# Another split of the pairs that take three cycles: ten, two and five, seven products

## The chip, the core and the metric

The kernel runs on one NeuronCore of a Trainium2 chip. Its engines run side by side and wait for each other through semaphores: PE (matmul, with its weight loads listed apart as PEld), DVE (vector), ACT (scalar), POOL (general purpose) and SP, whose queue issues the DMAs. The metric is the time of one execution on the device in microseconds, lower is better. Three runs of the kernel before took 1713.72, 1713.96 and 1714.29 us; the median is 1713.96 us.

## What is computed

The input is one sequence of 2048 tokens with 512 features, all in f32. The reference, cut to what matters:

```python
xn = _layernorm(x)
qkv = (xn @ wqkv) -> q, k, v of 32 heads, 16 wide each
scores = einsum("bhqd,bhkd->bhqk", q, k) * 16 ** -0.5
s = (softmax(scores) @ v, heads side by side) @ wo            # attention over all 2048 keys
h = (xn @ w_gate) * (xn @ w_up)                               # 1792 wide
g = silu(h @ w_down)
out = x + s * g
```

## The kernel before

**Two streams of work on PE.** The attention is cut into 32 units (8 groups of four heads by 4 chunks of 512 queries), each with 16 tiles of 128 keys. One *position* is one head of one key tile of one unit: there are 2048. A position (`position`, `expo`, `score`) issues two matmuls: `t`, the scores that are exponentiated on ACT into a tile `e`, and `s`, the scores of the position 86 later, turned the other way round, of which DVE takes the row maxima with one `tensor_reduce` (`mx`). The two use 64 rows of PE's array each, one the lower and one the upper half, and run side by side.

The second stream is everything else that PE must do once the first unit runs: projections of q and k, the gated layer and its down projection. These come as *pairs* (`pair`): two sums of products, each accumulated in a PSUM bank of its own (`misc`, two banks). A matrix product in split precision is a list of terms; 12 terms for one result at a contraction of 512, 15 for a down projection over five blocks of 128 features. The contraction of each term is cut in two halves of 64 rows: the lower half for one result runs beside the upper half for the other. One such step of two matmuls is called a *product* here (one `yield 1`). A pair has two halves of 12 or 15 products. In the first, the lower rows go to result 0 and the upper rows to result 1; in the second it is the other way round. So that the two halves of the array do not write the same bank at once, a one-element ACT copy (`look`, L294) reads result 1 between the two halves: the first product of the second half waits for it.

**Cycles.** The program is laid out by a planner in the Python code, and the order on every engine is the order of the program. A *cycle* takes two key tiles of a unit through: some positions, products between them, and then a *block* (`block`, L645), the matmuls `pv` that multiply the exponentials of eight positions with V; they use 128 rows and 32 columns each. ACT copies the block's result out (`part` at L656, `acc` at L651 for the first block of a unit). There are 256 cycles; 240 of them carry pairs.

**Banks.** PSUM has eight: three for `s`, three for `t` and the block's result together (tag `st`), two for `misc`. They are given out in turn. A position's `s` therefore needs the reduce of the position three before to be done. Behind a block the order of tag `st` is block, t of place 0, t of place 1, t of place 2, t of place 3: the t of place 2 needs the block's result copied out, and the t of place 3 needs the exponential of place 0 done. Place 0 is the first position of a cycle.

**The planner** is the class `Filler`. `fetch` runs when a half of a pair begins; for the first half it asks how many cycles the pair gets (`spread(n)`, 2 to 4, by the share of all products) and fills `queue` with the number of products of each cycle. With three cycles the middle one holds the end of the first half and the start of the second, as a tuple (`split`, `more`). `begin` takes the next entry; the main loop then chooses the number of positions:

```python
fits = min(9, max(7, int(2.6 + 0.62 * work))) if q + LEAD < TOTAL and work else 8
need = 8 * (b + 1)
last = min(max(q + fits, need + AHEAD[0]), need + AHEAD[-1], TOTAL - 4)
```

so that positions run one to four ahead of what the block needs. `Filler.spread` makes `plan`, the number of products behind each position of the cycle; `part` issues them. `share(n, gaps)` spreads n evenly, larger shares first. Between cycles `values` issues what reads the finished pair out of its banks (`before_values`: one DVE multiply for the gated layer at L357; two DVE additions, L428, for the down projection of the second and third group of blocks, one copy for the first), then the block, then what POOL has to split.

`soon`, `step` and `later` delay loads, splits and the silu by a count of positions, not of products.

Of the kernel before, what the change touches and what calls it, by code (L numbers as in the profile page):

```python
# [48 lines left out]
def body(ctx, tc, x, wqkv, wo, wg, wu, wd, out):  # L49
# [62 lines left out]
    def banks_of(bufs):  # L112
        stack = ExitStack()
        fst["ps"] = stack.enter_context(tc.tile_pool(name="ps" + "".join(bufs), bufs=1, space=PSUM, reuse_waits="tile")), bufs
        return stack
# [15 lines left out]
    def flush():  # L131
        while waiting:
            waiting.pop(0)[1]()
# [8 lines left out]
    def run_all(queue):  # L142
        while queue:
            queue.pop(0)()
# [309 lines left out]
    def prepare():  # L454

        done = [(NG - 1) * NC + c in finished for c in range(NC)]
        if 0 not in ops:
            if done[0] and fst.get("wo") == ND - 1:
                o_split(0, small_tiles())
        for c in (1, 2):  # L460
            if c not in ops and done[c] and ("big", c) in fst:
                h, l = fst["big", c]
                o_split(c, [(h[:, d], l[:, d]) for d in range(ND)])
        if 3 not in ops and "first" in fst:
            o_split(3, small_tiles())
# [171 lines left out]
    def block(todo):  # L637

        i = todo[0][0]
        g = i // NC  # L640
        o = psum("st", f"pv{i}")
        for n, (_, kt, es) in enumerate(todo):
            for j in range(4):
                h0 = (4 * g + j) * VW
                nc.tensor.matmul(o[32 * j:32 * j + 32], V[:, kt, h0:h0 + 32], es[j],  # L645
                                 start=n == 0, stop=n == len(todo) - 1)
        if todo[-1][1] == NT - 1 and i == NU - 1:
            last_heads(o)
        elif todo[0][1] == 0:
            sums[i] = keep.tile([P, 512], F32, name="acc", bufs=2)  # L650
            nc.scalar.activation(sums[i], o, AF.Copy)  # L651
        elif now[0] > NU * NT - LEAD // 4:
            nc.vector.tensor_tensor(sums[i], o, sums[i], op=OP.add)
        else:
            part = part_tile()
            nc.scalar.activation(part, o, AF.Copy)  # L656
            pool.tensor_tensor(sums[i], sums[i], part, op=OP.add)
# [43 lines left out]
    def run(gen):  # L701
        for _ in gen:
            pass
# [105 lines left out]
    def filler(wq0):  # L809
        yield from proj_pair(0, [(wq0, 0, 2), (wq0, 0, 3)])  # L810
        for m in range(1, NG // 2):
            wk, wq = fst["qk", m]
            for c in range(NC):
                if c == 2 and m + 1 < NG // 2:
                    fst["qk", m + 1] = qk_weights(m + 1, 1), qk_weights(m + 1, 0)
                yield from proj_pair(m, [(wk, 1, c), (wq, 0, c)])
                if m == 1 and c:
                    after = fst["high"].ins.name
                    for n, src in enumerate((xh, xl)):
                        put = sync.dma_start(XD[c][n].bitcast(F32), src[c].bitcast(F32))  # L820
                        tc.add_manual_dep(put.ins, after, BEHIND, reason="not before the first exponentials")
                if m == NG // 2 - 1 and c == NC - 2:
                    nxt = gu_weights(0)
        run_all(before_values)
        run_all(behind_values)
        flush()
        qkv.close()
        fst["fp"] = ffp.enter_context(tc.tile_pool(name="ffn", bufs=1, reuse_waits="tile"))
        yield from ffn(nxt)
# [5 lines left out]
    def step_small(q):  # L835
        if q and next(q[0], 1):
            q.pop(0)

    class Filler:
# [11 lines left out]
        def fetch(self):  # L851
            v = next(self.gen, self)
            if v is self:
                self.done = True
            elif v:
                k, n = v
                self.left = n
                if k == 0:
                    self.whole, odd = divmod(self.cycles(2 * n), 2)
                    self.split = max(2, round(n / (2 * self.whole + 1))) if odd else 0  # L860
                    self.more = max(2, self.split - 1) if odd and self.whole else n if odd else 0
                    self.queue = self.share(n - self.split, self.whole) if self.whole else []
                    if odd:
                        self.queue.append((self.split, self.more))
                    if self.whole:
                        self.queue += self.share(n - self.more, self.whole)
# [7 lines left out]
            return sum(both)  # L874

        def spread(self, gaps):
            if isinstance(self.now, tuple):
                a, b = self.now
                self.plan = self.share(a, 2) + [0] + self.share(b, gaps - 3)
            else:  # L880
                self.plan = self.share(self.now, gaps)

        def part(self):
            n = self.plan.pop(0) if self.plan else 0
# [14 lines left out]
    def values(rounds):  # L899
        if before_values:  # L900
            run_all(before_values)
        else:
            step_small(heads)
        run_all(reduced)
        block(rounds)
        run_all(behind_values)
        if rounds[-1][1] == NT - 1:
            heads.append(finish(rounds[0][0]))
            step_small(heads)
# [3 lines left out]
    def position(q):  # L913

        n, j = divmod(q, 4)
        i, kt = divmod(n, NT)
        g, c = divmod(i, NC)
        now[0] = n
        Tied.on = n < 18
        if j == 0:  # L920
            if kt == 8 and i + 2 < NU:
                load_q(i + 2)
            if kt == 0 and g + 1 < NG and c == 1:
                load_k(g + 1)
            ready[n] = i, kt, []
        if j == 3 and kt % 4 == 2:
            gates.append(lambda: step_small(later))
        ready[n][2].append(expo(i, kt, j))
        scored = q + LEAD
        if scored < TOTAL:  # L930
            score(scored, 1)
        step()
        if j == 1:
            prepare()
        if scored < TOTAL and scored % (4 * NT) == 4 * NT - 1:
            reduced.append(lambda: maxima(scored // (4 * NT)))
# [3 lines left out]
    with tc.manual_schedule(engines=ORDERED):  # L940
        with banks_of(EARLY_BUFS):
            fil = Filler(filler(early()), spread)
        ctx.enter_context(banks_of(BUFS))
        run(fst["v"])
        q = 0
        while q < 4:
            position(q)
            q += 1
        for b in range(NU * NT // 2):
            if fil.done:  # L950
                parts = iter([3, 2, 3, 2, 2, 2, 1, 2])
                fil = Filler(ending(), lambda n: next(parts))
            work = fil.begin()
            if b >= NU * NT // 2 - 2:
                last = TOTAL - 4 * (NU * NT // 2 - 1 - b)
            else:
# [3 lines that stand above are left out]
            count = last - q  # L960
            fil.spread(max(2, count - 2))
            for k in range(count):
                if k == count - 1:
                    run_all(gates)
                position(q)
                q += 1
                if 0 < k < count - 1 or count < 3:
                    fil.part()
            if b < NU * NT // 2 - 1:
                values([ready.pop(2 * b), ready.pop(2 * b + 1)])  # L970
        run_all(before_values)
        run_all(gates)
        while heads:
            step_small(heads)
        block([ready.pop(NU * NT - 2), ready.pop(NU * NT - 1)])
        run_all(behind_values)
        flush()
        while fil.left or not fil.done:
            now[0] += 1
            prepare()  # L980
            if not fil.left:
                fil.fetch()
            for _ in range(fil.left):
                next(fil.gen)
            fil.left = 0
            fil.fetch()
            flush()
# [17 lines left out]
```

## Time and profile before

| | |
|---|---|
| median of three runs | 1713.96 us |
| the profiled execution | 1715.28 us |
| its span, first to last instruction | 1713.4 us |
| ACT busy | 1309.0 us, 76% |
| POOL busy | 884.9 us, 52% |
| DMA, mean over the span | 85 GB/s |

The profile shows one execution. In a timeline a row is: start in us, duration in us, engine, source line, operation, output <- input, shapes, count; equal instructions that follow each other are merged into one row with the time from the first start to the last end, or for back-to-back ones their sum. In brackets stands how long the engine sat idle before and what ended it. Matmuls of 512 columns are listed with about 0.39 us each but follow each other on one half of the array every 0.23 us, since they are pipelined; PE's busy share says little for that reason, and the distance between starts says much.

### The profile page before, as it was taken

To read this page: it belongs to the slowest core of one execution; us is meant where nothing else is said; L and a number is where in the kernel's file an instruction comes from. 1 tells how busy PE (TensorE), PEld (TensorE's weight loads), DVE (VectorE), ACT (ScalarE), POOL (GpSimd) and SP (SyncE) were. 2 spreads that over 40 slices of the span, in tenths; PEclk is the share of its full clock that TensorE was granted. 3 is DMA by queue.
4 is the path that set the end of the run, shared out by engine and by line. 5 is a ranking of instruction groups with operands and counts; after the bars stand their busy time and mean duration, and the time that the engine had idled before them with its cause. 6 is when DMAs were issued, how large, how long until landed. Compare 5 with 4: busy or idle time off the path is not lost. (4 is left out here: it accounts for less than half of the span.)

```text
span 1713.4 us, 35012 instructions
## 1 busy us (share of the span) xinstructions
PE 1701.9 (99%) x13574; PEld 1043.7 (61%) x13574; DVE 1430.9 (84%) x2478; ACT 1309.0 (76%) x2568; POOL 884.9 (52%) x890
## 2 busy tenths in 40 slices
PE   8999999999999999999999999999999999999998
PEld 5666656666666666666656665666666566666655
DVE  6788888888888888888888888888888888888933
ACT  6357777777877778788777887877778787777774
POOL 5314444763653647446354572663637546446672
PEclk9999999999999999999999999999999999999999
DMA  6316633620241222412115220330225112011352
GB/s 209 108 40 193 248 126 117 153 72 13 71 91 36 82 72 67 96 41 61 36 49 136 65 72 24 87 76 27 60 84 122 54 36 73 27 54 47 123 178 78
DMA packets 117378, 145.79 MB, mean 85 GB/s; under 512 B 12636, under 2 KB 74332, under 8 KB 114524
## 3 DMA queue, kind: packets, MB, share of 16 engines
q1 hardware_dynamic: 117212, 143.55, 29.0%
q8 instruction: 107, 1.75, 0.4%
q14 instruction: 59, 0.48, 0.1%
HBM read 95.94 MB, written 47.45 MB: 84 GB/s over the span
## 5 line engine op out<-in xcount | busy, mean ns | idle before, releaser
L612 DVE TENSOR_REDUCE mx<-s 128x1 f32<-128x512 f32 x2048 | 1256.1, 683 | 212.4 <-PE s L610 178.1
L634 ACT ACTIVATE e<-t 128x512 f32<-128x512 f32 x2048 | 1101.3, 601 | 97.8 <-PE pv L645 46.6
L632 PE MATMUL t<-qs,ks 50*128 50x512 f32 x2048 | 782.3, 408 | 0.1
L610 PE MATMUL s<-ks,qs 48*128 48x512 f32 x2048 | 768.1, 409 | 0.6 <-DVE mx L612 0.5
L63 POOL TENSOR_TENSOR acc<-acc,part 128x512 f32<-128x512 f32 x214 | 276.1, 1290 | 588.8 <-ACT part L656 588.4
L632 PEld LDWEIGHTS t<-qs,ks 50*128 50x128 f32 x2048 | 359.2, 185 | 270.7 <-issue 110.2
L645 PE MATMUL pv<-e,V 128*32 128x512 f32 x4096 | 492.5, 598 | 0.0
L610 PEld LDWEIGHTS s<-ks,qs 48*128 48x128 f32 x2048 | 350.8, 185 | 28.2 <-issue 5.6
L656 ACT ACTIVATE part<-pv 128x512 f32<-128x512 f32 x214 | 128.1, 599 | 205.1 <-PE pv L645 205.1
L645 PEld LDWEIGHTS pv<-e,V 128*32 128x32 f32 x4096 | 107.0, 109 | 242.3 <-issue 216.9
L290 PE MATMUL g<-fh,w1h 64*128 64x512 f32 x224 | 90.5, 404 | 0.0
L286 PE MATMUL u<-fh,w0h 64*128 64x512 f32 x224 | 90.5, 404 | 0.0
L290 PE MATMUL y<-dh,hh 64*128 64x512 f32 x224 | 89.5, 400 | 0.0
L286 PE MATMUL y<-dh,hh 64*128 64x512 f32 x224 | 88.9, 397 | 0.0
L290 PE MATMUL u<-fh,w0l 64*128 64x512 f32 x224 | 88.2, 394 | 0.0
L290 PE MATMUL g<-fl,w1h 64*128 64x512 f32 x224 | 88.1, 393 | 0.0
L286 PE MATMUL u<-fh,w0l 64*128 64x512 f32 x224 | 88.0, 393 | 0.0
L290 PE MATMUL g<-fh,w1l 64*128 64x512 f32 x224 | 88.0, 393 | 0.0
L286 PE MATMUL g<-fl,w1h 64*128 64x512 f32 x224 | 88.0, 393 | 0.0
L286 PE MATMUL g<-fh,w1h 64*128 64x512 f32 x224 | 87.9, 392 | 0.0
L290 PE MATMUL u<-fl,w0h 64*128 64x512 f32 x224 | 87.8, 392 | 0.0
L286 PE MATMUL g<-fh,w1l 64*128 64x512 f32 x224 | 87.8, 392 | 0.0
(262 smaller groups left out, 2982.7 us busy)
## 6 DMA issues: line engine op xcount, KB each, us to landing
w1r<-in_wg_dram SPq DMA_DIRECT2D x56, 256.0 KB
w0r<-in_wu_dram SPq DMA_DIRECT2D x56, 256.0 KB
wdr<-in_wd_dram SPq DMA_DIRECT2D x56, 256.0 KB
qs<-QD SPq DMA_DIRECT2D x64, 192.0 KB
ks<-KD SPq DMA_DIRECT2D x12, 768.0 KB
KD<-hl SPq DMA_DIRECT2D x16, 512.0 KB
QD<-hl SPq DMA_DIRECT2D x16, 512.0 KB
OD<-acc SPq DMA_DIRECT2D x31, 256.0 KB
```

The lines of the kernel that those rows point to most:

```text
L63: got = getattr(self.engine, name)(*args, **kw)
L286: nc.tensor.matmul(outs[k], l[LOWER], r[LOWER], start=k == 0 and n == 0, stop=(stop or k == 0) and n == len(low) - 1, skip_group_check=k == 1)
L290: nc.tensor.matmul(outs[1 - k], l[UPPER], r[UPPER], start=k == 0 and m == 0, stop=(stop or k == 0) and m == len(high) - 1, skip_group_chec ...
L610: nc.tensor.matmul(o, QS[i][b:b + KB, pr, t * P:(t + 1) * P], k[b:b + KB, pr, kc * 512:(kc + 1) * 512], start=True, stop=True)
L612: nc.vector.tensor_reduce(MX[i][:, j, t, kc:kc + 1], o, axis=AX.X, op=OP.max)
L632: nc.tensor.matmul(o, k[b:b + KR, pr, kt * P:(kt + 1) * P], QS[i][b:b + KR, pr], start=True, stop=True)
L634: nc.scalar.activation(e, o, AF.Exp, scale=DH ** -0.5)
L645: nc.tensor.matmul(o[32 * j:32 * j + 32], V[:, kt, h0:h0 + 32], es[j], start=n == 0, stop=n == len(todo) - 1)
L656: nc.scalar.activation(part, o, AF.Copy)
```

## The change

The numbers of products of the three cycles, and the places of the products in the middle cycle, are changed. For a pair with 12 products a half: before 8, then 4 and 3, then 9; after 10, then 2 and 5, then 7. With 15: before 10, then 5 and 4, then 11; after 12, then 3 and 6, then 9. In the middle cycle the rest of the first half stood behind the second and third position, with one place free before the second half; now it stands whole behind the first position, two places are left free, so that three positions lie between the halves. For that, products may now be issued behind the first position too; plans that do not want it begin with a 0, which gives them the order that they had. Pairs of two and of four cycles keep theirs.

```diff
                 if k == 0:
                     self.whole, odd = divmod(self.cycles(2 * n), 2)
-                    self.split = max(2, round(n / (2 * self.whole + 1))) if odd else 0
-                    self.more = max(2, self.split - 1) if odd and self.whole else n if odd else 0
+                    self.split = 0 if not odd else n if not self.whole else 2 if n < 15 else 3
+                    self.more = 0 if not odd else n if not self.whole else (n - 2) // 2 if n < 15 else n * 2 // 5
                     self.queue = self.share(n - self.split, self.whole) if self.whole else []
...
         def spread(self, gaps):
-            if isinstance(self.now, tuple):
-                a, b = self.now
-                self.plan = self.share(a, 2) + [0] + self.share(b, gaps - 3)
+            if not isinstance(self.now, tuple):
+                self.plan = [0] + self.share(self.now, gaps)
+            elif self.now[0] < 4:
+                self.plan = [self.now[0], 0, 0] + self.share(self.now[1], gaps - 2)
             else:
-                self.plan = self.share(self.now, gaps)
+                self.plan = [0] + self.share(self.now[0], 2) + [0] + self.share(self.now[1], gaps - 3)
...
-                if 0 < k < count - 1 or count < 3:
+                if k < count - 1:
                     fil.part()
```

## The prediction

> **What bounds the kernel now.** I read the page first, then the list of waits, then the timeline of single cycles.
>
> ```profile
> span 1713.4 us, 35012 instructions
> ...
> PE 1701.9 (99%) x13574; PEld 1043.7 (61%) x13574; DVE 1430.9 (84%) x2478; ACT 1309.0 (76%) x2568; POOL 884.9 (52%) x890
> ...
> L612 DVE TENSOR_REDUCE mx<-s 128x1 f32<-128x512 f32 x2048 | 1256.1, 683 | 212.4 <-PE s L610 178.1
> L634 ACT ACTIVATE e<-t 128x512 f32<-128x512 f32 x2048 | 1101.3, 601 | 97.8 <-PE pv L645 46.6
> ```
>
> PE has almost no gap, and DVE's largest idle time is spent waiting for PE. So a cycle lasts as long as PE's steps in it, plus whatever PE waits. The list of waits shows the one that the change moves:
>
> ```profile
> PEld u L286 <- ACT look L294: 5.8, 25, 0.2
> PEld y L286 <- ACT look L294: 3.6, 16, 0.2
> PEld p L286 <- ACT look L294: 1.4, 6, 0.2
> ```
>
> 25 + 16 + 6 = 47 waits; by the planner's arithmetic 48 pairs take three cycles before the ending (35 with 12 products a half, 13 with 15). One such middle cycle, four and three products, in the timeline (`pv` begins a block):
>
> ```profile
> 764.34 1.93 PE L645 MATMUL pv<-e,V 128*32 128x512 f32 x16
> ...
> 766.20 0.50 PE L632 MATMUL t<-qs,ks 50*128 50x512 f32 x1
> ...
> 766.39 0.60 ACT L656 ACTIVATE part<-pv 128x512 f32<-128x512 f32 x1 [1.35 <-PE pv L645]
> 766.54 0.39 PE L632 MATMUL t<-qs,ks 50*128 50x512 f32 x1
> ...
> 766.77 3.68 DVE L612 TENSOR_REDUCE mx<-s 128x1 f32<-128x512 f32 x6 [1.29 <-PE t L632]
> ...
> 766.89 1.57 ACT L634 ACTIVATE e<-t 128x512 f32<-128x512 f32 x3
> ...
> 768.18 0.40 PE L632 MATMUL t<-qs,ks 50*128 50x512 f32 x1
> 768.32 0.14 ACT L294 ACTIVATE look<-u 1x1 f32<-1x1 f32 x1
> ...
> 768.53 0.18 PEld L286 LDWEIGHTS u<-fh,w0h 64*128 64x128 f32 x1 [0.23 <-ACT look L294]
> 768.53 0.49 PE L286 MATMUL u<-fh,w0h 64*128 64x512 f32 x1
> ...
> 768.87 0.39 PE L286 MATMUL u<-fl,w0h 64*128 64x512 f32 x1
> ...
> 769.57 0.39 PE L610 MATMUL s<-ks,qs 48*128 48x512 f32 x1
> 769.89 0.16 PEld L645 LDWEIGHTS pv<-e,V 128*32 128x32 f32 x8 [0.37 <-ACT e L634]
> ```
>
> The look runs behind three exponentials, ends at 768.46, and 0.07 us later the weight load starts. A matmul whose weights load late is listed from the load, but the next one on that half follows after 0.34 us, not 0.23: it counts as started 0.11 later. Without the wait the second product would have stood at 768.18 + 2 x 0.23 = 768.64; it stands at 768.87. **One stall costs 0.23 us.**
>
> Block starts around other kinds of cycle give their lengths:
>
> ```profile
> 708.84 1.92 PE L645 MATMUL pv<-e,V 128*32 128x512 f32 x16
> 714.23 1.93 PE L645 MATMUL pv<-e,V 128*32 128x512 f32 x16
> ...
> 725.77 1.92 PE L645 MATMUL pv<-e,V 128*32 128x512 f32 x16
> 732.04 1.92 PE L645 MATMUL pv<-e,V 128*32 128x512 f32 x16
> 738.11 1.93 PE L645 MATMUL pv<-e,V 128*32 128x512 f32 x16
> 744.84 1.92 PE L645 MATMUL pv<-e,V 128*32 128x512 f32 x16
> 751.81 1.92 PE L645 MATMUL pv<-e,V 128*32 128x512 f32 x16
> 758.78 1.49 PE L645 MATMUL pv<-e,V 128*32 128x512 f32 x12
> ...
> 769.89 1.92 PE L645 MATMUL pv<-e,V 128*32 128x512 f32 x16
> 775.94 1.50 PE L645 MATMUL pv<-e,V 128*32 128x512 f32 x12
> ```
>
> By the plan these are: 7 products with 7 positions, 5.39 (708.84 to 714.23); 10 with 8, 6.27; five and four with 8, 6.07; 11 with 9, 6.73; 12 with 9, 6.97; then 8 with 7, 5.56 (758.78 to 764.34); four and three with 7, 5.55; 9 with 8, 6.05. A step more costs 0.23 (8 with 7 against 12 with 9: six steps, 1.41). So a cycle of n steps takes about 2.08 + 0.233 n: 14 steps want 5.34. The middle cycle of 12 loses 0.21, that of 15 (17 steps, 6.04 wanted) 0.03, the cycle of 7 with 7 loses 0.05. **All that the change can take away is 35 x 0.21 + 13 x 0.03 = 7.7 us, or 0.45%.**
>
> **The change part by part.** The number of positions, products and blocks stays; over three cycles 12-pairs keep 22 positions (8, 7, 7 for 7, 7, 8). No DMA is moved against the positions, since loads and splits are delayed by counts of positions; SP's and POOL's queues keep their order. The plans of all other cycles keep theirs, as the leading 0 issues nothing; these edits cost nothing.
>
> *The look.* It now comes behind the first exponential alone. On ACT it takes 0.05 us of its turn (768.32 to the next exponential, by the spacing of the first three: 1.57 less 0.60, halved, is 0.49); the exponential of place 1 has its scores later than that, which hides it. Counted from the first position (766.20 is 0): exponential 0 runs from 0.69 to 1.29, so the look ends near 1.32, and the second half's first product may load from 1.39. It would stand behind place 3, not before 1.5. So this stall goes.
>
> *What is late next.* With two products behind place 0, PE's steps stand at 0.34 and 0.57 (products), 0.81, 1.04 and 1.27 (places 1, 2, 3). Place 3 needs the reduce and the exponential of place 0. What such a wait costs is seen in a cycle with few products, 7 with 8 positions, that runs into DVE:
>
> ```profile
> 722.21 4.28 DVE L612 TENSOR_REDUCE mx<-s 128x1 f32<-128x512 f32 x7 [0.67 <-PE s L610]
> ...
> 724.15 0.18 PEld L610 LDWEIGHTS s<-ks,qs 48*128 48x128 f32 x1
> 724.15 0.50 PE L610 MATMUL s<-ks,qs 48*128 48x512 f32 x1
> ...
> 724.49 0.39 PE L290 MATMUL y<-dl,hh 64*128 64x512 f32 x1
> ...
> 725.35 0.18 PEld L610 LDWEIGHTS s<-ks,qs 48*128 48x128 f32 x1
> ```
>
> Reduces follow each other every (4.28 - 0.68) / 6 = 0.60. The third ends at 722.21 + 1.20 + 0.68 = 724.09, and place 5's load starts at 724.15; the fifth ends at 725.29, and place 7's starts at 725.35: 0.06 behind the reduce both times, and 0.11 more until the matmul counts. So a place cannot count as started before the end of the reduce (or exponential) three places back plus 0.17.
>
> *Middle cycle of 12.* Reduce 0 runs from 0.57 to 1.25, exponential 0 to 1.29: place 3 counts from 1.46, against 1.27. Loss 0.19. Later places are not held: reduce 1 starts when its scores are there, 0.46 behind place 1 (0.57 less the 0.11 of a late load), at 1.27, ends at 1.95, allows place 4 at 2.12, and that comes at 1.46 + 3 x 0.23 = 2.16; place 6 is allowed at 3.32 and comes at 3.33. Eight steps and 0.32 to the block (769.57 to 769.89): 1.46 + 1.87 + 0.32 = 3.65, with the 1.86 before the first position (764.34 to 766.20) **5.51**, against 5.55. Bounds: 5.34 with no wait; 5.60 if the late restart hits both halves of the array one after the other (another 0.1). I take 5.51, since both releases are rows.
>
> *12-pair.* Before 5.56 + 5.55 + 6.05 = 17.16; after 6.27 + 5.51 + 5.39 = 17.17 by these rows, and 17.14 by the line 2.08 + 0.233 n with the losses 0, 0.17 and 0.05. The first cycle's kind comes as 6.25 to 6.27, so I take -0.02. **35 x -0.02 = -0.7 us** (bounds: 5.34 makes it -6.6, 5.60 makes it +2.5).
>
> *Middle cycle of 15.* Products at 0.34, 0.57, 0.81, places 1 to 3 at 1.04, 1.28, 1.51, two products, place 4 wanted at 2.21, one, place 5 at 2.68, two, place 6 at 3.38, one, place 7 at 3.85, the block at 4.17. DVE has only reduce 0 until place 1's scores come at 1.50; it then runs 1.50, 2.10, 2.70, 3.30. Place 4 counts from 2.18 + 0.17 = 2.35 (+0.14), place 5 from 2.78 + 0.17 = 2.95 (+0.27), place 7 from 3.98 + 0.17 = 4.15 (+0.30). The cycle takes 1.86 + 4.15 + 0.32 = **6.33** against 6.07. Bounds 6.03 and 6.45. With the first and last cycle: before 6.27 + 6.07 + 6.73 = 19.07, after 6.97 + 6.33 + 6.05 = 19.35; by the line, +0.24. I take 0.26: **13 x 0.26 = +3.4 us** (bounds -0.5 and +4.9).
>
> *The end of a pair.* A shorter last cycle leaves DVE less time before the next pair wants the banks. Where two additions must empty them, before:
>
> ```profile
> 613.61 1.92 PE L645 MATMUL pv<-e,V 128*32 128x512 f32 x16
> ...
> 614.78 1.28 DVE L428 TENSOR_TENSOR y<-y,y 128x512 f32<-128x512 f32 x2
> ...
> 620.74 1.49 PE L645 MATMUL pv<-e,V 128*32 128x512 f32 x12
> ```
>
> That pair ended with 9 products and 8 positions, and the cycle behind it took 7.13, not 6.97: 0.16 lost. After the change the eight 15-pairs of the second group end in just that cycle; before, they ended in 11 products, 0.47 later, and lost little. The four 12-pairs of the third group end with 7 and 7, 0.06 worse. **8 x 0.15 + 4 x 0.06 = +1.4 us** (bounds 0 and 2.0). The pairs of the gated layer have one multiply and stay covered.
>
> **The sum:** -0.7 + 3.4 + 1.4 = **+4.1 us**: 1719.4 for the profiled execution of 1715.28, which lies 1.3 above the median; on the median 1718.1, I say **1718**.
>
> *A rule against the change.* The granted clock stays whole over cycles with such short waits:
>
> ```profile
> 700.00:780.00 80.00, 80.00 (x660) 48.55 (x658) 69.16 (x118) 63.42 (x127) 32.83 (x33) 1.00 0.29 61
> ```
>
> Behind the five engines stands the clock, 1.00. The Trainium skill, "TensorE: Matmul & The Clock Gate", section "A second HAM failure mode: psum-queue depth-cycling", tells of a kernel with 512 columns whose short waits on PSUM banks made the clock swing between half and full. By that rule the new waits at place 3 would bring half clock; by the row they do not, and the sum stands.
>
> **The rivals.**
> 1. *The banks are free in time* (faster). If place 3 finds reduce 0 and exponential 0 done, the look's stall goes and nothing takes its place: -6.6 - 0.5 + 1.4 = -5.7, 1708. For it: the wait at the look is a real one. Against it: reduce 0 would have to end 0.15 earlier and exponential 0 0.19 earlier than in the rows. It decides as soon as place 3 comes at 1.46 or later.
> 2. *Waits add up on both halves* (slower by more): 2.5 + 4.9 + 2.0 = +9.4, 1723. For it: the 15-pairs' middle cycle has three waits; against it: in the rows above the other half ran on.
> 3. *A draw*: the 15-pairs' middle cycle, whose pattern no row shows, waits only once, 6.17 in place of 6.33; +4.1 - 2.1 = +2.0, 1716. For it: DVE idles up to 1.50 and has room.
> 4. *Half clock* during the middle cycles: 14 x 0.233 = 3.3 us more in each of 48, +157 us, 1871. The row's 1.00 speaks against it.
>
> That the change does nothing is excluded by the plan: other numbers are issued.
>
> **How the numbers follow.** My forecast 0.53, rival 1 0.12, rival 2 0.16, rival 3 0.18, rival 4 0.01. A change under 0.2% (3.4 us) could not be told from none. Faster: most of rival 1, 0.11. Within: rival 3 and the lower part of the forecast, 0.38. Slower: 0.51. Range 1711 to 1722: it takes in the draw and leaves out most of rival 1 and the tail of rival 2; the forecast alone reaches from 1715 to 1720.
>
> **What would show it.** Right: waits of PE's loads for the look fall from 47 to a few; middle cycles of 12 near 5.5 with place 3's load just behind exponential 0; middle cycles of 15 at 6.3; last cycles at 5.39 and 6.05; the cycles behind 15-pairs of the second group 0.15 longer. Wrong: middle cycles of 12 at 5.34 (rival 1), of 15 at 6.17 or less (rival 3), or waits in the first cycles, where I expect none.

## The result, and the profile after

The changed kernel takes 1719.53 us (median of 7, 1719.18 to 1720.19) against 1714.44 us (7 runs, 1713.72 to 1715.36): ratio 1.003, 95% interval 1.002 to 1.004. It is 5.1 us slower by the medians; the two profiled executions, 1719.69 and 1715.28 us, lie 4.4 us apart, and what follows accounts for those. Times without a unit are in us. A 12-pair is a pair with 12 products a half, a 15-pair one with 15; places are counted from 0.

The page after, first and busy line:

```profile
span 1717.9 us, 34963 instructions
...
PE 1706.4 (99%) x13574; PEld 1054.4 (61%) x13574; DVE 1435.4 (84%) x2478; ACT 1313.4 (76%) x2568; POOL 886.2 (52%) x890
```

The engines' instruction counts are those of before, and PE shows 99% again: from these lines nothing can be told. The difference is in the distances between blocks. With the starts of all blocks, as in the prediction, the 239 cycles that follow the first block can be sorted by their place in the plan. "The line" is 2.10 + 0.2315 n for a cycle of n steps (products and positions together), close to the prediction's 2.08 + 0.233 n; it meets the cycles without a wait within 0.02:

| cycles | count | mean before | mean after | difference in all |
|---|---|---|---|---|
| middle cycle of 12-pairs | 35 | 5.549 | 5.506 | -1.5 us |
| their first and last cycles, but for 4 below | 66 | 0.01 over the line | 0.03 over the line | +1.3 us |
| middle cycle of 15-pairs | 13 | 6.087 | 6.325 | +3.1 us |
| cycles behind the 8 pairs of the second group | 8 | 0.05 over the line | 0.25 over the line | +1.6 us |
| all others | 117 | | | +0.3 us |

These give 4.8; the work ahead of the first block was 0.5 shorter in this execution and that behind the last of these 239 cycles 0.2 longer, which makes the 4.5 us between the spans 1717.9 and 1713.4. The last part holds two more pairs of three cycles, which the change alters too and for which the prediction has no term.

A middle cycle of 12 after the change, in the timeline (`pv` begins a block):

```profile
541.32 1.92 PE L645 MATMUL pv<-e,V 128*32 128x512 f32 x16
...
543.17 0.49 PE L632 MATMUL t<-qs,ks 50*128 50x512 f32 x1
...
543.74 3.79 DVE L612 TENSOR_REDUCE mx<-s 128x1 f32<-128x512 f32 x6 [1.19 <-PE s L610]
...
543.86 0.59 ACT L634 ACTIVATE e<-t 128x512 f32<-128x512 f32 x1
...
544.34 0.14 ACT L294 ACTIVATE look<-u 1x1 f32<-1x1 f32 x1
...
544.50 0.18 PEld L632 LDWEIGHTS t<-qs,ks 50*128 50x128 f32 x1 [0.30 <-ACT look L294]
544.51 0.50 PE L632 MATMUL t<-qs,ks 50*128 50x512 f32 x1
...
544.85 0.39 PE L286 MATMUL u<-fh,w0h 64*128 64x512 f32 x1
...
546.82 0.16 PEld L645 LDWEIGHTS pv<-e,V 128*32 128x32 f32 x8 [0.24 <-issue]
```

The look is done at 544.48, and the first product of the second half (L286 at 544.85) follows place 3 without a wait of its own. But place 3's weight load starts only at 544.50, 1.33 behind place 0 at 543.17, and the step after it comes 0.34 later: the stall has moved from the look to place 3. The first exponential ends at 544.45, the first reduce at 543.74 + 0.69 = 544.43. The list of waits blames the look:

```profile
PEld t L632 <- ACT look L294: 10.7, 36, 0.3
```

The mean of 5.506 holds one cycle of 5.751, from 440.19, in which the copy of the block's result came late and held place 2 as well; the other 34 have 5.499.

In the last cycle of these pairs, 7 products with 7 positions, the reduces on DVE set the pace at the end:

```profile
549.24 3.68 DVE L612 TENSOR_REDUCE mx<-s 128x1 f32<-128x512 f32 x6 [1.11 <-PE s L610]
...
551.78 0.18 PEld L610 LDWEIGHTS s<-ks,qs 48*128 48x128 f32 x1
```

The fourth reduce ends at 549.24 + 1.80 + 0.68 = 551.72, and the load of place 6, three places on, starts at 551.78. These cycles take 5.40 on the mean where the line gives 5.34; before, the last cycles stood 0.02 over the line. That makes up the +1.3 us.

A middle cycle of 15:

```profile
502.99 1.92 PE L645 MATMUL pv<-e,V 128*32 128x512 f32 x16
...
504.84 0.49 PE L632 MATMUL t<-qs,ks 50*128 50x512 f32 x1
...
505.41 0.69 DVE L612 TENSOR_REDUCE mx<-s 128x1 f32<-128x512 f32 x1 [1.59 <-PE s L610]
...
506.35 3.68 DVE L612 TENSOR_REDUCE mx<-s 128x1 f32<-128x512 f32 x6 [0.25 <-PE t L632]
...
507.10 0.18 PEld L610 LDWEIGHTS s<-ks,qs 48*128 48x128 f32 x1
...
507.69 0.18 PEld L610 LDWEIGHTS s<-ks,qs 48*128 48x128 f32 x1
...
508.89 0.18 PEld L610 LDWEIGHTS s<-ks,qs 48*128 48x128 f32 x1
...
509.31 0.16 PEld L645 LDWEIGHTS pv<-e,V 128*32 128x32 f32 x8 [0.24 <-issue]
```

DVE's second reduce starts 0.94 behind the first, since three products stand between place 0 and place 1; the usual distance is 0.60. From there every reduce is 0.34 late. The second reduce ends at 507.03 and place 4's load starts at 507.10; the third ends at 507.63, place 5's at 507.69; the fifth at 508.83, place 7's at 508.89.

And the ends of the two pairs of a second group. The block at 515.33 closes the last cycle of the first of them, the block at 534.62 that of the second; 522.25 and 541.32 each end the cycle behind it:

```profile
515.33 1.92 PE L645 MATMUL pv<-e,V 128*32 128x512 f32 x16
...
516.53 1.28 DVE L428 TENSOR_TENSOR y<-y,y 128x512 f32<-128x512 f32 x2
...
517.75 2.54 DVE L612 TENSOR_REDUCE mx<-s 128x1 f32<-128x512 f32 x4
...
517.85 0.18 PEld L290 LDWEIGHTS y<-dh,hh 64*128 64x128 f32 x1
...
522.25 1.92 PE L645 MATMUL pv<-e,V 128*32 128x512 f32 x16
...
534.62 1.92 PE L645 MATMUL pv<-e,V 128*32 128x512 f32 x16
...
535.80 1.28 DVE L428 TENSOR_TENSOR y<-y,y 128x512 f32<-128x512 f32 x2
536.99 0.20 DVE L616 TENSOR_REDUCE mm<-mx 128x16 fp32r<-128x64 f32 x1
...
537.72 0.65 DVE L612 TENSOR_REDUCE mx<-s 128x1 f32<-128x512 f32 x1
...
541.32 1.92 PE L645 MATMUL pv<-e,V 128*32 128x512 f32 x16
```

Behind the block at 515.33 the additions end at 517.81, 2.48 later, and the load of the next pair's first product in the upper half starts at 517.85, just behind them. The cycle lasts 6.92 where its 20 steps want 6.73. Behind the block at 534.62 the additions end 2.46 later, as late as behind the block at 613.61 of the prediction (2.45). Here four small operations that finish a unit's maxima (`mm` and what follows it) stand behind them too, and push the cycle's first reduce to 3.10 behind the block, where it is 2.42 behind the block at 515.33. The cycle lasts 6.70 where its 18 steps want 6.27.

### The profile page after: what moved, and what is told of

Same layout as the page of the kernel before. It is cut to its first block, busy times and chain, and to the rows that moved or that the text cites. A ratio compares the mean times of both kernels' runs of the same rounds, so it can differ in the third digit from the quotient of the medians.

```text
span 1717.9 us, 34963 instructions
## 1 busy us (share of the span) xinstructions
PE 1706.4 (99%) x13574; PEld 1054.4 (61%) x13574; DVE 1435.4 (84%) x2478; ACT 1313.4 (76%) x2568; POOL 886.2 (52%) x890
## 5 line engine op out<-in xcount | busy, mean ns | idle before, releaser
L610 PE MATMUL s<-ks,qs 48*128 48x512 f32 x2048 | 778.6, 413 | 0.6 <-DVE mx L612 0.5
L290 PE MATMUL y<-dh,hh 64*128 64x512 f32 x224 | 88.7, 396 | 0.0
L286 PE MATMUL u<-fh,w0l 64*128 64x512 f32 x224 | 88.0, 393 | 0.0
L286 PE MATMUL g<-fh,w1l 64*128 64x512 f32 x224 | 87.9, 392 | 0.0
L290 PE MATMUL u<-fl,w0h 64*128 64x512 f32 x224 | 87.9, 392 | 0.0
L286 PE MATMUL g<-fl,w1h 64*128 64x512 f32 x224 | 87.9, 392 | 0.0
L286 PE MATMUL y<-dl,hh 64*128 64x512 f32 x224 | 87.9, 392 | 0.0
L286 PE MATMUL g<-fh,w1h 64*128 64x512 f32 x224 | 87.8, 392 | 0.0
L286 PE MATMUL u<-fl,w0h 64*128 64x512 f32 x224 | 87.8, 392 | 0.0
```

The source lines that it names most:

```text
L286: nc.tensor.matmul(outs[k], l[LOWER], r[LOWER], start=k == 0 and n == 0, stop=(stop or k == 0) and n == len(low) - 1, skip_group_check=k == 1)
L290: nc.tensor.matmul(outs[1 - k], l[UPPER], r[UPPER], start=k == 0 and m == 0, stop=(stop or k == 0) and m == len(high) - 1, skip_group_chec ...
L610: nc.tensor.matmul(o, QS[i][b:b + KB, pr, t * P:(t + 1) * P], k[b:b + KB, pr, kc * 512:(kc + 1) * 512], start=True, stop=True)
```

## The experiments

### Which pairs make the loss

Only the 12-pairs changed, the 15-pairs with the numbers and places of before:

```diff
-self.split = ... 2 if n < 15 else 3
-self.more = ... (n - 2) // 2 if n < 15 else n * 2 // 5
+self.split = ... 2 if n < 15 else 5
+self.more = ... (n - 2) // 2 if n < 15 else 4
```

> Theory (12-pairs even, the loss is the 15-pairs'): the 12-pairs alone cost nothing, since the place-3 wait (0.16) and the last cycle of 7 with 7 (0.05) together take back the 0.21 of the look; with some 0.1 for the banks behind four down projections the time is 0 to +0.7 us against before. The middle cycles of 12 last 5.50, those of 15 6.09 again. Rival (the new place-3 wait makes the loss): +3 to +5 us here.

Measured: 1714.10 us (10 runs) against 1714.58 (17 runs), ratio 0.9996, interval 0.9986 to 1.0005. No difference shows, since the interval includes 1; the middle value lies just outside what was expected, on the fast side. Middle cycles of 12 last 5.499, of 15 6.075.

Only the 15-pairs changed:

```diff
-self.split = ... 2 if n < 15 else 3
-self.more = ... (n - 2) // 2 if n < 15 else n * 2 // 5
+self.split = ... 4 if n < 15 else 3
+self.more = ... 3 if n < 15 else n * 2 // 5
```

> Theory: the 13 pairs with 15 products carry the loss: 13 x 0.25 = 3.2 us in their middle cycles (6.33 against 6.09) and 1.3 to 1.7 us behind the eight pairs that end in two additions: +4.5 to +5 us against before. Middle cycles of 12 back at 5.55. Rival (the 12-pairs make it): under +1 us.

Measured: 1719.27 us (8 runs) against 1714.58, +4.7 us, ratio 1.003, interval 1.0019 to 1.0040. Middle cycles of 15 last 6.327, of 12 5.548. So **the 13 pairs with 15 products carry the loss, and the 35 pairs with 12, most of what was changed, come out even.**

### What place 3 waits for

The look of the 12-pairs' middle cycle is issued one position later, so that it stands behind the exponential of place 1 on ACT:

```diff
             if k == 0:
-                nc.scalar.activation(look, outs[1][0:1, 0:1], AF.Copy)
+                late = lambda o=outs[1]: nc.scalar.activation(look, o[0:1, 0:1], AF.Copy)
+                late_look.append(late) if fst.get("late") else late()
...
                 position(q)
+                run_all(late_look)
                 q += 1
                 if k < count - 1:
+                    fst["late"] = isinstance(fil.now, tuple) and fil.now[0] == 2 and k == 0
                     fil.part()
+                    fst["late"] = False
```

> All of the change, but in the middle cycle of 12 the look is put behind the exponential of place 1 on ACT instead of that of place 0. Theory (place 3 waits for the exponential of place 0): place 3's weight load stays at 3.19 us behind the start of the block and the first product of the second half waits for the look instead, at about 3.8 in place of 3.53: the cycles last 5.8 in place of 5.50, +10 us. Rival (place 3 waits for the look, as the list of waits names it): place 3's load itself moves to about 3.75, and the cycles last 6.05 or more, +19 us.

Measured in one execution: 1730.91 us, 11.2 more than the profiled execution of the change; the middle cycles of 12 last 5.845. One of them in the timeline (line numbers are one or two higher here):

```profile
544.05 1.92 PE L647 MATMUL pv<-e,V 128*32 128x512 f32 x16
...
546.60 1.15 ACT L636 ACTIVATE e<-t 128x512 f32<-128x512 f32 x2
...
547.24 0.18 PEld L634 LDWEIGHTS t<-qs,ks 50*128 50x128 f32 x1 [0.30 <-ACT e L636]
...
547.64 0.14 ACT L295 ACTIVATE look<-u 1x1 f32<-1x1 f32 x1
...
547.84 0.18 PEld L287 LDWEIGHTS u<-fh,w0h 64*128 64x128 f32 x1 [0.41 <-ACT look L295]
```

Place 3's load starts 3.19 behind the block at 544.05, as it does in the change (541.32 to 544.50: 3.18), although the look now runs 0.40 behind it. So **place 3 does not wait for the look; the name in the list of waits was wrong**, as it was put down to what ended last before the load. A load that does wait for the look starts 0.06 behind its end here (547.78 to 547.84); 0.02, as in the change, was too soon to be one. The load that waits is that of `t`, which needs the exponential of place 0, and in the change it starts 0.05 behind that one's end (544.45 to 544.50). The reduce of place 0, which `s` needs, ends only 0.02 earlier; how long it would hold place 3 without the exponential was not tried.

### Why the middle cycle of 15 is slow

The three products stand behind place 1 instead of place 0:

```diff
             if not isinstance(self.now, tuple):
                 self.plan = [0] + self.share(self.now, gaps)
+            elif self.now[0] == 3:
+                self.plan = [0, 3, 0] + self.share(self.now[1], gaps - 2)
             elif self.now[0] < 4:
```

> All of the change, but in the middle cycle of 15 the three products stand behind place 1 instead of place 0. Theory (DVE starts its second reduce late when products stand ahead of place 1): the second reduce starts 0.60 behind the first instead of 0.94, the waits at places 4, 5 and 7 are gone, and one wait for the look, now behind two exponentials, takes their place, about 0.24: these cycles last 6.27 in place of 6.325, 0.7 us in all. Rival (it is the number of products, three and six, that costs): waits at places 4 and 5 stay, 6.3 or more, plus the look's.

Measured in one execution: 1717.48 us, 2.2 less than the change's profiled 1719.69; the middle cycles of 15 last 6.228, 0.097 less, which is 1.3 us in all 13.

```profile
502.15 1.92 PE L645 MATMUL pv<-e,V 128*32 128x512 f32 x16
...
504.58 4.28 DVE L612 TENSOR_REDUCE mx<-s 128x1 f32<-128x512 f32 x7 [1.59 <-PE t L632]
...
505.65 0.14 ACT L294 ACTIVATE look<-y 1x1 f32<-1x1 f32 x1
...
505.85 0.18 PEld L286 LDWEIGHTS y<-dh,hh 64*128 64x128 f32 x1 [0.32 <-ACT look L294]
...
508.39 0.16 PEld L645 LDWEIGHTS pv<-e,V 128*32 128x32 f32 x8 [0.37 <-ACT e L634]
```

Seven reduces run in one piece, (4.28 - 0.68) / 6 = 0.60 apart; the look's wait is back, behind two exponentials. The numbers three and six are the same as in the change: what made the waits at places 4, 5 and 7 was that the three stood ahead of place 1. The gain is nearly twice what was expected, as the cycles stand 0.19 over the line with the look's wait, and not 0.24. The 0.9 us by which the whole execution gained more than these cycles is within what single executions differ by (1719.18 to 1720.19 for the change).

### The banks behind two additions

The eight 15-pairs of the second group leave out the addition of their first result; the even token tiles of every chunk miss that part of y.

```diff
                         if ti == n == 0:
                             add()
-                        else:
+                        elif ti != 1 or n:
                             before_values.append(add)
```

> All of the change, but the eight pairs with 15 products of the second group leave out one of their two additions (the tokens of every first result miss that part of y). Theory (the banks are free too late behind two additions): the cycles behind these pairs, which lose 0.17 to 0.45 after the change, lose 0 to 0.2: -1.4 to -1.9 us against the change. Rival (the late banks are the ACT's or the block's): no difference, under 0.3 us.

Measured in one execution: 1718.19 us, 1.5 less than the change's profiled 1719.69. The same stretch as above:

```profile
515.63 1.92 PE L645 MATMUL pv<-e,V 128*32 128x512 f32 x16
522.35 1.92 PE L645 MATMUL pv<-e,V 128*32 128x512 f32 x16
...
534.70 1.92 PE L645 MATMUL pv<-e,V 128*32 128x512 f32 x16
...
535.89 0.68 DVE L428 TENSOR_TENSOR y<-y,y 128x512 f32<-128x512 f32 x1
...
540.98 1.92 PE L645 MATMUL pv<-e,V 128*32 128x512 f32 x16
```

6.72 in place of 6.92, and 6.28 in place of 6.70. Over the eight cycles it is 1.8 us. So DVE's additions were what held seven of them. The eighth, from 1166.34 here, still lasts 6.89: its load of place 2 waits for the block's copy on ACT, as it does after the change, so there the rival holds.

### A version that beats both

If the look is late only because it stands behind an exponential that does not concern it, it can be put ahead of that one. The numbers and places are those of the kernel before; in the middle cycle of 12 the exponential of place 2 is issued behind the products that follow place 2, and so behind the look:

```diff
         e = etile()
-        nc.scalar.activation(e, o, AF.Exp, scale=DH ** -0.5)
+        if fst.get("hold"):
+            held.append(lambda: nc.scalar.activation(e, o, AF.Exp, scale=DH ** -0.5))
+        else:
+            nc.scalar.activation(e, o, AF.Exp, scale=DH ** -0.5)
         return e
...
+                fst["hold"] = isinstance(fil.now, tuple) and fil.now[0] == 4 and k == 2
                 position(q)
+                fst["hold"] = False
                 q += 1
                 if k < count - 1:
                     fil.part()
+                run_all(held)
```

> The kernel before (eight, four and three, nine products; places as before), but in the middle cycle of 12 the look is put ahead of the exponential of place 2 on ACT, not behind it. Theory (the look is late because it stands behind three exponentials): the look starts when the first half's products are done, 0.15 earlier, the first product of the second half waits 0.08 in place of 0.23, and exponentials 2 and 3 come 0.35 later, which costs up to 0.05 at places 5 and 6: middle cycles 5.43 to 5.48 in place of 5.55, -2.5 to -4 us against before. Rival (later exponentials hold the t of places 5 and 6 by as much as was gained): no gain, or slower by up to 2 us.

Measured: 1710.56 us (11 runs, 1710.25 to 1711.78) against 1714.63 (15 runs), ratio 0.9978, interval 0.9969 to 0.9987: **4.1 us faster than the kernel before and 9 faster than the change.** Middle cycles of 12 last 5.447, 0.10 less than before; 35 x 0.10 = 3.6 us. The whole gain lies at the far end of what was expected, and the 0.5 us beyond these cycles is less than single executions differ by.

```profile
537.89 1.92 PE L649 MATMUL pv<-e,V 128*32 128x512 f32 x16
...
540.44 1.08 ACT L638 ACTIVATE e<-t 128x512 f32<-128x512 f32 x2
...
541.70 0.16 ACT L295 ACTIVATE look<-u 1x1 f32<-1x1 f32 x1 [0.18 <-PE u L291]
...
541.76 0.57 ACT L636 ACTIVATE e<-t 128x512 f32<-128x512 f32 x1
...
541.91 0.18 PEld L291 LDWEIGHTS g<-fh,w1h 64*128 64x128 f32 x1
541.96 0.44 PE L291 MATMUL g<-fh,w1h 64*128 64x512 f32 x1
541.99 0.41 PE L287 MATMUL u<-fh,w0h 64*128 64x512 f32 x1
...
542.25 0.40 PE L291 MATMUL g<-fl,w1h 64*128 64x512 f32 x1
...
542.39 0.18 PEld L633 LDWEIGHTS t<-qs,ks 50*128 50x128 f32 x1 [0.18 <-ACT e L636]
...
543.34 0.16 PEld L649 LDWEIGHTS pv<-e,V 128*32 128x32 f32 x8 [0.29 <-ACT e L638]
```

The look now waits for PE, 0.18, and starts 3.81 behind the block, not 3.98 as in the cycle shown before (764.34 to 768.32). The second half's first two products start 0.29 apart on the upper half of the array (541.96 and 542.25) and 0.26 on the lower (541.99 and 542.25), and not 0.34. The held exponential (L636 here) ends at 542.33 and releases place 5's load at 542.39; that costs little, as the step was due at about 542.48.

## Why the prediction was right

The forecast was 4.1 us slower, 1718; it came out at 5.1 by the medians and 4.4 by the profiled executions it was summed against. The mechanism held: the look's wait went, the banks three places back took its place, the 15-pairs lost by a late second reduce, and the ends of pairs lost a little more. That the sum came so close is luck in part: single terms are off by 0.3 to 0.5 us and cancel, and executions of one kernel differ by 1 us.

- **That the look's stall goes** holds: no load of the second half's products (L286) waits for it in these cycles. The prediction would have read it from the count of waits for the look falling from 47 to a few; that sign failed, as 36 waits, now of place 3, are still put down to it. The start of place 3's load with the look moved away showed the right cause.
- **The middle cycle of 12**: 5.51 forecast, 5.506 measured, with place 3's load behind place 0's exponential, as said. The 12-pairs together: -0.7 forecast, -0.2 in the profile (-1.5 in the middle, +1.3 in the first and last cycles); alone they were 0.5 faster than before, within the interval. The -0.7 rested on a slip in adding: the line 2.08 + 0.233 n with the losses 0, 0.17 and 0.05 gives 17.18 for the three cycles, not 17.14, so line and rows both say +0.01 a pair where -0.02 was taken. That makes +0.4 us, and the sum +5.2.
- **The middle cycle of 15**: 6.33 forecast, 6.325 measured, with the late second reduce and the loads at places 4, 5 and 7 behind it. The term was 3.4; it is 3.1. ("By the line, +0.24" is a slip as well: the line gives +0.26, which is what was taken.)
- **The ends of pairs**: +1.4 forecast, +1.7 in the profile (1.6 behind the second group and 0.1 behind the third, where 0.06 a pair was taken and 0.03 measured). What was missed is that the maxima of a unit fall behind the additions in two of the eight cycles; there additions and maxima together cost 0.44 a cycle, not 0.16. They stand there before the change too, at 0.15.
- **The rivals.** That the banks are free in time: no, place 3 waits in the middle cycles. That waits add up on both halves of the array: no, this wanted 5.60 and 6.45 for the middle cycles, and they have 5.506 and 6.325. That the 15-pairs wait only once: no, the loads of places 4 and 5 wait for reduces in each of the 13, and that of place 7 in the one shown. Half clock: no; with waits in every one of the 48 middle cycles the granted clock of the profiled execution after the change is 0.999, and in the middle cycle of 12 shown above it is 1.00 (the third number from the end of its row):

```profile
core 0: 1717.9 us, clock 0.999
...
541.32:546.82 5.50, 5.50 (x45) 3.14 (x45) 4.29 (x8) 4.17 (x10) 3.92 (x4) 1.00 0.35 100
```

- The direction was given at 0.51 against 0.38 for no change that could be told. More could not be had from the sum: in the 12-pairs a gain and a loss of about 7 us each stand against each other, and 0.03 us a cycle is 1 us in 35.

## What to carry to other kernels

Before a stall is moved, work out what the next wait at the same place allows: here the look cost 0.21 a cycle, and the banks three places back cost 0.16 as soon as the look was out of the way. A list of waits names what ended last, not what was waited for; compare the time between the two with a wait that is certain, or move the suspect. Where a small instruction is late because of its place in an in-order queue, move it within that queue first, and leave the other engines' order as it is: that gave 4.1 us, where moving the matmuls of the same pairs gave nothing that could be told.

## What was not expected of the hardware

Where a weight load had to wait and started together with its matmul, the next step on that half of the array came about 0.34 us behind, and not 0.23 (544.51 to 544.85 above). The matmul's listed start does not show these 0.11 us. Of 123 such pairs of steps after the change, away from the blocks, nine in ten lie between 0.334 and 0.343 us. Where the load started 0.05 to 0.08 ahead of the matmul, as in the fastest version, it was 0.29 and 0.26.

The spacing of products and places was so even that, with one distance for each engine and the 0.11, the mean lengths of the two kinds of middle cycle came out within 0.01 us, while the whole execution varies by 1 us from run to run.
